# Two masks copied from the identity on VectorE in place of three selects on GpSimd, and one load of x moved from unit 48 of a kernel to its start

## The chip, the cores and the metric

The kernel runs on one core of a Trainium2 chip. The metric is device time in microseconds (us) of one execution; quoted times are medians over several executions, with their number. A profiled execution also gives a span, from the first to the last thing the trace records, which is shorter than the timed figure of the same execution (716.6 beside 718.46 for the kernel before).

Engines: PE is TensorE (matmul), PEld its weight load, DVE VectorE, ACT ScalarE, POOL GpSimd, SP SyncE. An issue is the instruction that starts a transfer; a transfer lands when its last semaphore update is made. A fetch is a transfer that brings the next instructions of an engine's list.

## The reference, cut to what matters

```python
# x (8, 4096, 192) fp32, weight (8 heads, 7 taps), w_in (192, 2048), w_out (2048, 192)
w = softmax(weight, axis=-1)                 # per head
x_pad = six zero rows before each of the 8 sequences
y[b, s, head] = sum_k w[head, k] * x_pad[b, s + k, head]     # causal, depthwise
h = y.reshape(32768, 192) @ w_in
g = where(h > 0, h, exp(min(h, 0)) - 1)      # ELU
out = g @ w_out
```

## The kernel before

The 32768 rows are cut into 32 "supers" of 1024 rows, four to a sequence. Each super has 16 column blocks of w_in, times two halves of 512 rows; one such pair is a "unit", so there are 1024 units. For each unit PE makes H (three matmuls of 512 columns), ACT takes the exponential E of it, POOL clamps E to at most 1, DVE forms gT = max(E - 1, H), and PE multiplies gT into the output banks. The convolution is done for later supers by matmuls with a banded matrix in between. POOL also issues most loads.

GpSimd's program is one list. It makes masks, issues the first loads, and then clamps unit after unit; loads of later x (`x_before`) and the zeroing of the six padding rows at the start of a new sequence (`batch_zeros`) stand between clamps:

```python
X3_AT = (0, 48)     # the two halves of x of super 3: before which unit they are issued
ZERO_AT = 8         # column block in which the padding rows are zeroed
...
for gr in range(2):
    x_before.setdefault(X3_AT[gr], []).append((NXB, gr))
...
g.memset(ones[:], 1.0).then_inc(s_id)
...                                    # ident: one affine_select
for step in range(2):                  # owner: two affine_selects
...                                    # block8: one more
load_w_in(0)                           # three issues each
load_w_in(1)
load_w_out(0)
for gr in range(2):
    load_x(1, gr)
load_w_out(1)
load_w_out(2)
for gr in range(2):
    load_x(2, gr)
for i, (n, u) in enumerate(units):
    s, at_n = divmod(i // 2, NQ)
    if i % 2 == 0 and at_n == ZERO_AT and (s + 2) % SPB == 0 and s + 2 < NS:
        batch_zeros(s + 2)
    for to_load in x_before.get(i, ()):
        load_x(*to_load)
    W(s_exp, i + 1)
    g.tensor_scalar(out=E[:, i % NE, :], in0=E[:, i % NE, :],
                    scalar1=1.0, scalar2=0.0, op0=ALU.min, op1=ALU.max).then_inc(s_clp)
```

The masks are used by the softmax of the weights: `owner` spreads a head's taps over its channels (a matmul on PE), `block8` makes a block diagonal on DVE:

```python
# VectorE, at the start
v.memset(zw[:], 0.0).then_inc(s_zw)
v.memset(wband[:], 0.0).then_inc(s_wb)
v.memset(xbh[:, :, :, :], 0.0).then_inc(s_xz)
W(s_wb, 1)
W(s_wq, 16)                                   # the weights have landed
v.tensor_reduce(wmx[:], wq[:], AXIS.X, ALU.max).then_inc(s_set)
...                                           # subtract, sum, reciprocal, multiply
v.tensor_tensor(wnb[:], block8[:], wn[:, :].unsqueeze(1).to_broadcast([...]), ALU.mult)
```

## Time and profile before

| kernel before | |
|---|---|
| median | 718.48 us (3 executions, 718.13 to 719.18) |
| span of the profiled execution | 716.6 us |
| PE busy | 710.7 us, 99% |
| 62 issues of x loads on POOL | 54.7 us, 884 ns each |
| 1024 clamps on POOL | 603.0 us busy, 611 ns each (they overlap a little, so one per 0.59 us) |

Columns are line, engine, operation, output and input with their shape, count, busy time and mean ns of one, and how long that engine idled before it and for whom.

```profile
L714 POOL TENSOR_SCALAR E<-E 128x512 f32<-128x512 f32 x1024 | 603.0, 611 | 41.1 <-ACT E L760 34.2
L871 DVE SCALAR_TENSOR_TENSOR gT<-E,H 128x512 f16<-128x512 f32 x1024 | 631.8, 681 | 62.8 <-POOL E L714 58.4
```

DVE idles 62.8 us, and 58.4 us of that is waiting for POOL's clamps; POOL itself idles only 41.1 us before its clamps. A unit takes about 0.68 us (1024 units in some 700 us), and POOL can clamp one per 0.59 us (603.0 / 1024), so it has some 0.09 us to spare per unit. Each x issue of 0.88 us therefore puts POOL behind, and by this estimate it needs some 9 or 10 units to catch up.

### The profile page before, as it was taken

The page shows a single profiled execution, that of the slowest core. Times are in us where ns is not written, and L with a number is a line of the kernel's source. Part 1 is how long each engine was busy: PE and PEld are TensorE (multiplying, and loading weights), DVE is VectorE, ACT ScalarE, POOL GpSimd, SP SyncE. Part 2 cuts the span into 40 slices and gives each one's busy share as a digit, 9 for nine tenths or more (in the row PEclk, how much of TensorE's full clock was granted, in tenths as well). Part 3 has the DMA queues.
Part 4 walks back from the last instruction along what each step waited for, and adds up shares of the span by engine and source line. Part 5 has one row for each costly group of instructions (what it writes and reads, how often), then busy time and mean ns, then how long its engine had stood idle before and what let it go on. Part 6 is the DMA issues. An engine that isn't in the chain of part 4 may idle for free.

```text
span 716.6 us, 27662 instructions
## 1 busy us (share of the span) xinstructions
PE 710.7 (99%) x11873; PEld 681.6 (95%) x11873; DVE 641.5 (90%) x1049; ACT 677.4 (95%) x1290; POOL 663.6 (93%) x1112
## 2 busy tenths in 40 slices
PE   8999999999999999999999999999999999999998
PEld 4699999999999999999999999999999999999998
DVE  7999889998898998899998999988989988999994
ACT  6999999999999999999999999999999999999994
POOL 9999999999999999999999999999999999999893
PEclk9999999999999999999999999999999999999999
DMA  9635334564433544444554344544445534444212
GB/s 183 99 72 95 65 73 78 93 86 76 80 79 74 95 89 64 80 85 79 87 91 69 73 76 95 87 73 76 85 73 91 93 63 78 87 80 83 63 43 69
DMA packets 132303, 58.80 MB, mean 82 GB/s; under 512 B 98374, under 2 KB 131412, under 8 KB 132180
## 3 DMA queue, kind: packets, MB, share of 16 engines
q0 software_dynamic: 43504, 16.77, 22.4%
q1 hardware_dynamic: 88388, 39.37, 22.0%
q8 instruction: 93, 1.52, 0.9%
q10 hardware_dynamic: 288, 0.88, 0.4%
q14 instruction: 30, 0.25, 0.1%
HBM read 34.63 MB, written 25.46 MB: 84 GB/s over the span
## 4 chain that ended last, share of the span: by engine, by line
PE 96%; POOL 2%; ACT 1%; DVE 0%; issue 0%; DVEq 0%; POOLq 0%
PE H L1052 54%; PE H L1029 37%; PE H L1004 4%; POOL xg L631 1%; ACT E L760 1%; POOL E L714 1%; POOL w_in L651 0%; POOL w_out L662 0%; DVE gT L871 0%; ACT csb L756 0%; POOL owner L679 0%; DVE osb L862 0%; POOL block L689 0%; POOL ident L668 0%; POOL ones L666 0%
## 5 line engine op out<-in xcount | busy, mean ns | idle before, releaser
L871 DVE SCALAR_TENSOR_TENSOR gT<-E,H 128x512 f16<-128x512 f32 x1024 | 631.8, 681 | 62.8 <-POOL E L714 58.4
L1029 PE MATMUL H<-att,w_in 64*128 64x512 bf16 x3072 | 679.8, 376 | 1.2 <-DVE gT L871 0.9
L1052 PE MATMUL H<-w_out,gT 64*128 64x192 f16 x8192 | 680.4, 243 | 0.1
L714 POOL TENSOR_SCALAR E<-E 128x512 f32<-128x512 f32 x1024 | 603.0, 611 | 41.1 <-ACT E L760 34.2
L1052 PEld LDWEIGHTS H<-w_out,gT 64*128 64x128 f16 x8192 | 606.7, 94 | 17.5 <-PE H L1052 1.5
L760 ACT ACTIVATE E<-H 128x512 f32<-128x512 f32 x1024 | 585.0, 601 | 23.9 <-PE H L1029 0.4
L1029 PEld LDWEIGHTS H<-att,w_in 64*128 64x128 bf16 x3072 | 275.3, 93 | 7.8 <-DVE gT L871 2.9
L1004 PE MATMUL H<-xg,Tm 64*128 64x240 bf16 x496 | 90.9, 263 | 0.0
L756 ACT ACTIVATE csb<-H 112x480 bf16<-112x480 f32 x124 | 70.7, 570 | 0.4 <-PE H L1004 0.3
L767 ACT ACTIVATE osb<-H 128x384 f32<-128x384 f32 (+1 forms) x129 | 62.0, 482 | 6.9 <-PE H L1052 6.8
L631 POOL DMA_DIRECT2D xg<-in_x_dram x62 | 54.7, 884 | 0.2 <-issue 0.2
L1004 PEld LDWEIGHTS H<-xg,Tm 64*128 64x128 bf16 x496 | 42.6, 94 | 1.2 <-DVE gT L871 0.3
L862 DVE COPY osb<-H 128x192 f32<-128x192 f32 x1 | 0.4, 357 | 7.3 <-PE H L1052 7.3
L909 PE MATMUL H<-zw 128*128 128x512 bf16 x10 | 4.3, 588 | 1.2 <-DVE zw L775 1.2
L909 PEld LDWEIGHTS H<-zw 128*128 128x128 bf16 x10 | 1.2, 134 | 3.0 <-issue 1.7
L651 POOL DMA_DIRECT2D w_in<-in_moe_w_in_dram x6 | 3.6, 612 | 0.0
L736 ACT ACTIVATE xb<-xs 128x512 bf16<-128x512 f32 x2 | 1.2, 622 | 2.4 <-DMA xs<-in_x_dram 2.4
L978 PE MATMUL H<-xT,taps 64*64 64x256 bf16 (+1 forms) x50 | 2.6, 317 | 0.0
L662 POOL DMA_DIRECT2D w_out<-in_moe_w_out_dram x3 | 2.5, 853 | 0.0
L978 PEld LDWEIGHTS H<-xT,taps 64*64 64x64 bf16 x50 | 2.0, 106 | 0.5 <-issue 0.2
L729 ACT ACT_TABLE_LOAD x1 | 1.3, 1283 | 1.2 <-PEq L1119 1.2
L936 PEld LDWEIGHTS H<-ident,xb 64*64 64x64 bf16 x48 | 1.2, 126 | 0.8 <-ACT xb L736 0.8
(45 smaller groups left out, 20.5 us busy)
## 6 DMA issues: line engine op xcount, KB each, us to landing
out_dram<-osb SPq DMA_DIRECT2D x126, 192.0 KB, 2.9
xg<-in_x_dram POOLq DMA_DIRECT2D x61, 240.0 KB, 4.5
xs<-in_x_dram ACTq DMA_DIRECT2D x1, 768.0 KB, 4.6
w_in<-in_moe_w_in_dram POOLq DMA_DIRECT2D x6, 128.0 KB, 4.7
att<-csb SPq DMA_TRANSPOSE x31, 3.9
w_out<-in_moe_w_out_dram POOLq DMA_DIRECT2D x2, 192.0 KB, 7.9
w_out<-in_moe_w_out_dram POOLq DMA_DIRECT2D x1, 384.0 KB, 11.8
w_in<-w_in SPq DMA_DIRECT2D x1, 336.0 KB, 6.8
```

The lines of the kernel that those rows point to most:

```text
L631: g.dma_start(xg[0:rows, b, 2 * w0 + gr : 2 * w1 : 2, :], src).then_inc(s_x[b][gr], 16)
L651: g.dma_start(w_in[0:HP, j, c0:c1], bass.AP(tensor=moe_w_in.tensor, offset=8 * j * FF + c0, ap=[[CPH * FF, HEADS], [FF, 8], [1, c1 - c0]], ...
L714: g.tensor_scalar(out=E[:, i % NE, :], in0=E[:, i % NE, :], scalar1=1.0, scalar2=0.0, op0=ALU.min, op1=ALU.max,).then_inc(s_clp)
L756: a.activation(*conv_evac(W, m), ACT.Copy).then_inc(s_ce)
L760: a.activation(E[:, i % NE, :], H[:, bank_of[item], :], ACT.Exp).then_inc(s_exp)
L767: a.activation(*out_evac(W, *item[1:]), ACT.Copy).then_inc(s_oev[item[2]])
L871: v.scalar_tensor_tensor(out=gT[:, s % NG3, q, u, :], in0=E[:, i % NE, :], scalar=1.0, in1=H[:, bank_of[item], :], op0=ALU.subtract, op1=A ...
L909: pe.matmul(H[:, bank, :], zw[:, 0:P], zw[:, 0:GS], start=True, stop=True)
L978: ins = pe.matmul(H[to, bank_of["d", j] + (j == 2 and c0 > 0), c0:c1], taps[rows, tap, rows], xT[rows, j, HALO - PAD + tap + c0 : HALO - P ...
L1004: ins = pe.matmul(H[:, bank_of["c", m], 256 * q : 256 * q + UC], Tm[rows, h, :], xg[rows, s % NXB, :, CPH * h : CPH * (h + 1)].rearrange(" ...
L1029: ins = pe.matmul(H[:, bank_of[item[:3]], :], w_in[HP * r : HP * (r + 1), j, FC * q : FC * (q + 1)], att[HP * r : HP * (r + 1), s % 2, j, ...
L1052: ins = pe.matmul(acc_of(k, g)[:, D * kb : D * (kb + 1)], gT[HP * rt : HP * (rt + 1), t % NG3, q, g, t0 : t0 + P], w_out[HP * rt : HP * (r ...
```

## The change

The intent: POOL's list at the start sets when the first clamp happens, so take three mask selects off it. `owner` and `block8` are both repeats of the 8 x 8 corner of the identity, so VectorE copies them from there, before the weights have landed. In the room gained, the second half of x of super 3 is issued at the start, so that no x issue stands at unit 48.

```diff
@@ -41,7 +41,7 @@
 WCOLS = ((0, 8 * FC), (8 * FC, 16 * FC))
 UPPER = ((0, FC), (FC, 2 * FC), (2 * FC, 4 * FC), (4 * FC, 8 * FC), (8 * FC, 16 * FC))
 WOUT = (0, 4, 8, 16)
-X3_AT = (0, 48)
+X3_AT = (0, 0)
 HALO = 8
 BW = P
 ON_DVE = 3
@@ -466,6 +466,7 @@
         s_scr = sema("s_scr")
         s_x = [[sema(f"s_x{i}_{g}") for g in range(2)] for i in range(NXB)]
         s_id = sema("s_id")
+        s_own = sema("s_own")
         s_xs = sema("s_xs")
         s_xh = sema("s_xh")
         s_wb = sema("s_wb")
@@ -674,27 +675,6 @@
                 base=0,
                 channel_multiplier=1,
             ).then_inc(s_id)
-            for step in range(2):
-                W(s_id, 2 + step)
-                g.affine_select(
-                    out=owner[:, :],
-                    in_=owner[:, :] if step else ones[0:HEADS, :],
-                    pattern=[[0, 2], [1 - 2 * step, HP]],
-                    compare_op=ALU.is_ge,
-                    fill=0.0,
-                    base=7 * step,
-                    channel_multiplier=8 * (2 * step - 1),
-                ).then_inc(s_id)
-            W(s_id, 4)
-            g.affine_select(
-                out=block8[:, :, :],
-                in_=ones[0:HEADS, 0 : HEADS * KSIZE].rearrange("p (h k) -> p h k", h=HEADS),
-                pattern=[[1, HEADS], [0, KSIZE]],
-                compare_op=ALU.is_equal,
-                fill=0.0,
-                base=0,
-                channel_multiplier=-1,
-            ).then_inc(s_id)
             load_w_in(0)
             load_w_in(1)
             load_w_out(0)
@@ -775,6 +755,18 @@
             v.memset(zw[:], 0.0).then_inc(s_zw)
             v.memset(wband[:], 0.0).then_inc(s_wb)
             v.memset(xbh[:, :, :, :], 0.0).then_inc(s_xz)
+            W(s_id, 2)
+            v.tensor_copy(
+                owner[:, :].rearrange("p (g h e) -> p g h e", g=2, e=8),
+                ident[0:HEADS, 0:HEADS]
+                .unsqueeze(1)
+                .unsqueeze(3)
+                .to_broadcast([HEADS, 2, HEADS, 8]),
+            ).then_inc(s_own)
+            v.tensor_copy(
+                block8[:, :, :],
+                ident[0:HEADS, 0:HEADS].unsqueeze(2).to_broadcast([HEADS, HEADS, KSIZE]),
+            ).then_inc(s_own)
             W(s_wb, 1)
             W(s_wq, 16)
             v.tensor_reduce(wmx[:], wq[:], AXIS.X, ALU.max).then_inc(s_set)
@@ -798,7 +790,7 @@
                 scalar2=None,
                 op0=ALU.mult,
             ).then_inc(s_set)
-            W(s_id, 5)
+            W(s_own, 2)
             W(s_set, 5)
             v.tensor_tensor(
                 wnb[:],
@@ -908,7 +900,7 @@
                     for _ in range(item[2]):
                         pe.matmul(H[:, bank, :], zw[:, 0:P], zw[:, 0:GS], start=True, stop=True)
                 elif item[0] == "s":
-                    W(s_id, 4)
+                    W(s_id, 2)
                     W(s_set, 6)
                     pe.matmul(
                         H[:, bank_of["d", 2], 0:KSIZE],
```

## The prediction

> **What bounds the kernel now.** I read four views of the kernel before, in this order: the busy shares of the page, the chain of waits over the whole span, the same chain in its first 46 us, and the matmul counts in stretches of 1 us around the one place where the chain leaves the PE late.
>
> First the page: busy shares, then the chain that ended last.
>
> ```profile
> PE 710.7 (99%) x11873; PEld 681.6 (95%) x11873; DVE 641.5 (90%) x1049; ACT 677.4 (95%) x1290; POOL 663.6 (93%) x1112
> ...
> PE 96%; POOL 2%; ACT 1%; DVE 0%; issue 0%; DVEq 0%; POOLq 0%
> ```
>
> The PE is busy 99% of the 716.6 us and carries 96% of the chain. Cut into stretches of 100 us between 100 and 600 us, it executes 1695 to 1697 matmuls in each and is never idle. So the middle of the kernel is a fixed amount of matmul work, and nothing in this change touches its matmuls. Only the 4% of the chain that is not PE can be won, and that lies at the two ends. What POOL has of the chain is in the first 46 us; columns are start, duration and what ran:
>
> ```profile
> 1.07 0.30 POOL ident L668
> 1.43 0.30 POOL owner L679
> 1.79 0.30 POOL owner L679
> 2.14 0.33 POOL block L689
> 2.48 0.73 POOL w_in L651
> ...
> 10.15 2.69 POOL xg L631 x3
> 12.86 0.64 POOL E L714
> 13.52 0.70 DVE gT L871
> 14.27 1.45 PE H L1029 x7
> ...
> 40.98 1.77 POOL E L714 x3
> 42.74 0.82 POOL xg L631
> 43.59 0.64 POOL E L714
> 44.26 0.70 DVE gT L871
> 45.00 0.28 PE H L1029
> ```
>
> Two things are to be seen. At the start the chain is POOL's own program, one item behind the other: four masks, then twelve issues of transfers, until POOL is free for the first clamp of E at 12.86. The PE then goes on at 14.27. At 42.74 the chain passes through POOL once more: one issue of x for super 3 (its second half) stands between two clamps, gT comes late and the PE's next H matmul waits for its bank until 45.00. After that the chain stays on the PE until the tail.
>
> What the second place costs I take from the counts of matmuls that touch each microsecond: H matmuls (512 columns) first, then the output matmuls (192 columns). The stretches are the same, 43 to 47.
>
> ```profile
> 43.00:44.00 1.00, 1.00 (x6) 1.00 0.55 184
> 44.00:45.00 1.00, 0.50 (x4) 1.00 0.82 85
> 45.00:46.00 1.00, 1.00 (x5) 1.00 1.33 156
> ...
> 43.00:44.00 1.00, 1.00 (x15) 1.00 0.55 184
> 44.00:45.00 1.00, 0.78 (x11) 1.00 0.82 85
> 45.00:46.00 1.00, 0.78 (x9) 1.00 1.33 156
> ```
>
> The convolution matmuls (240 columns) are 0, 2 and 2 there. In columns: 6 x 512 + 15 x 192 = 5952 in the full microsecond, 4 x 512 + 11 x 192 + 2 x 240 = 4640 in the next, 5 x 512 + 9 x 192 + 2 x 240 = 4768 in the third. Missing: 1312 + 1184 = 2496 of 5952 per us, which is 0.42 us of PE work. It is never made up, because the PE has no idle time afterwards.
>
> **What the Trainium skill says.** "DMA: Bandwidth & Descriptors", section "SWDGE vs HWDGE vs iDMA": a transfer issued from GpSimd has its descriptors computed in software on that engine. The trace agrees that this is POOL time: the 62 issues of xg take 884 ns each, the three in a row before the first clamp 2.73 us, 0.91 each. The same page, section "Queues, rings and completion order": one DMA engine alternates between its queues, and switches only after a whole packet of descriptors. That bears on w_in beside the first load of x; the trace of before cannot settle it, because the packets of the x load run from 1.84 to 5.04 and those of w_in only begin at 3.95. "SBUF — State Buffer", section "Who interferes with whom": a VectorE copy in a two-port mode locks GpSimd out for the whole instruction, descriptor writing included. The first w_in issue took 777 ns and the next five 562 to 600, beside small VectorE work; this fits, but does not prove it.
>
> **The change part by part.**
>
> Removed from POOL: three mask selects, from the start of the first at 1.43 to the first w_in issue at 2.43. That is 1.00 us. Nothing else stands there: POOL is not waiting for anything from 0.79 to 12.86.
>
> Moved on POOL: the issue of the second half of super 3 goes from before unit 48 (42.68) to before unit 0. It adds one issue, 0.91 us by the spacing of its neighbours. Net on POOL at the start: -1.00 + 0.91 = -0.09 us, so the first clamp comes at about 12.77. DVE, then PE, follow with the spacings of before, and the chain from there to 40 us is PE and ACT work with no wait for a transfer, so I let 0.1 us through to the end.
>
> At unit 48: ACT takes the exponential of this unit at 42.10. Where POOL is free, the clamp follows an exponential at 0.67 us after its start (ACT 24.07 to POOL 24.74), so at 42.77. POOL's clamps before it end by 42.74. So unit 48 goes at about 42.77 in place of 43.59, gT at 43.43 and the bank is free at 44.17 in place of 45.00. The PE finishes the work in front of it (two convolution matmuls from 44.01 and 44.12) about then, so the stall should go almost whole: -0.4 us. It cannot give the full 0.82 us of the issue, since the PE lost only 0.42.
>
> Added on DVE: two copies of 8x128 and 8x56 elements. Small DVE instructions follow each other here at 0.19 us (wmx 2.25, the subtraction 2.44); I take 0.22 each, 0.44 in all. DVE idles 0.26 us for the weights before wmx, so the softmax moves by about 0.2 us. It leads through taps and x to the first attention tile, the first H (10.55) and the first exponential (11.39). That last one could feed POOL at 11.39 + 0.67 = 12.06, and POOL will not be free until 12.77: 0.7 us of slack, more than 0.2. So it costs nothing at the end.
>
> The instructions and waits of PE, ACT and SP are the same in both kernels but for the PE's wait for the masks. Sum: -0.1 - 0.4 = -0.5 us, 718.48 - 0.5 = 718.0.
>
> **The rivals.**
>
> First: the earlier w_in issue slows the first load of x. ACT waits for that load until 5.44, and everything up to the first exponential hangs on it. For: w_in's issue comes 1.0 us sooner, at 1.4, while this 768 KB load is running. Against: the slack of 0.7 us, minus the 0.2 used by the masks. If the load slips by 1.0 us, the start gets 0.5 us worse, and the time is about 718.5.
>
> Second: the copies on VectorE hold up POOL's descriptor writing, or the thirteenth issue takes longer with so many transfers queued. Each would eat the net 0.09 and perhaps 0.3 more: 718.1 to 718.4.
>
> Third: the issue at 42.68 is hidden, or another wait takes its place. For: ACT is busy almost throughout (4.88 of 5 us between 40 and 45) and has no lead of its own to give. Against: ACT itself waited 0.31 us for the PE at 45.44, so ACT was then held up by this stall and not its cause. If it were so, 718.4.
>
> Fourth: the 240 KB added to the opening backlog of transfers, which drains at 24.84, lengthen it by about 1.3 us (super 3's first half took 190 GB/s there) to 26.1. The first transpose of attention is issued at 25.70 and lands at 29.94. I expect at most tenths, since the added load is last in its queue and w_out and super 1 and 2 stand before it.
>
> **Range and chances.** All four rivals move tenths of a microsecond; three runs of before lie from 718.13 to 719.18, so the noise is of the size of the gain. Without any gain and with high noise, 718.9; with both gains whole and low noise, 717.2. Two per cent is 14.4 us; nothing here is larger than 2 us. So: within 2% 0.98, 0.01 on each side.
>
> **What would show each step.** Right: the first w_in issue near 1.4; four xg issues in a row before a first clamp near 12.8; no gap of POOL, and no DVE idle of 0.75 us, near 43 to 44; PE counts without the dip at 44 to 46; steady counts of 1695 per 100 us as before; span about 716.1. Wrong: a first clamp later than 12.9 (second rival; or the first, if its idle time is put down to ACT), ACT waiting for x beyond 5.7, the same dip with another releaser (third), or attention landing later than 30.2 (fourth). If the PE is idle at a new place after 50 us, my claim that it is saturated falls.

## More of the kernel before

The output of each group of 256 or 128 rows is copied from its bank to SBUF and stored. SyncE issues every store but the last, ScalarE the last one; the copy before that one is on VectorE:

```python
# SyncE
elif item[1:] != (NK - 1, 1):
    evacuated_by(W, *item[1:])
    out_group(sy, *item[1:])
# ScalarE, after everything else
evacuated_by(W, NK - 1, 1)
out_group(a, NK - 1, 1)
```

## The result, and the profile after

| | before | changed |
|---|---|---|
| median | 718.40 us (6 executions, 718.13 to 719.18) | 719.06 us (6 executions, 718.46 to 719.57) |
| span of the profiled execution | 716.61 us | 717.00 us |

The ratio of times is 1.0008, with a 95% interval of 0.9995 to 1.0021. So the class, within 2%, was right; 719.06 lies outside the predicted range of 717.2 to 718.9, and the gain of 0.5 us is not there.

The two parts that the change aimed at did what they should. First the chain of waits of the changed kernel at the start (start, duration, what ran):

```profile
1.45 0.78 POOL w_in L652
...
9.15 3.41 POOL xg L632 x4
12.56 0.73 POOL E L694
13.32 0.70 DVE gT L863
14.06 1.45 PE H L1021 x7
```

The first w_in issue starts at 1.45 in place of 2.43. There are four x issues in a row, and then the first clamp at 12.56, against 12.86. PE goes on at 14.06, against 14.27: 0.21 us earlier, where 0.09 had been worked out.

The counts of H matmuls per microsecond at unit 48 (stretch, busy time of all, busy time and count of these matmuls, granted clock, DMA share, GB/s):

```profile
43.00:44.00 1.00, 1.00 (x6) 1.00 0.55 181
44.00:45.00 1.00, 0.95 (x5) 1.00 0.05 11
45.00:46.00 1.00, 1.00 (x6) 1.00 0.00 0
```

The output matmuls in the second of these microseconds:

```profile
44.00:45.00 1.00, 0.93 (x13) 1.00 0.05 11
```

With the four convolution matmuls there, it has 5 x 512 + 13 x 192 + 4 x 240 = 6016 columns, where before it had 4640. The dip is gone, and in the timeline of POOL the eight clamps there run without a break:

```profile
40.78 4.85 POOL L694 TENSOR_SCALAR E<-E 128x512 f32<-128x512 f32 x8 [0.29 <-ACT E L740]
```

To see where the gain went, the busy shares are of no use, since PE is busy 99% in both. What helps is that both kernels execute the same 11760 matmuls, from the first H on, in the same order but for neighbours. I took the start times of each from the two traces and subtracted. This is output of my own, not a view of the profile; negative means that the changed kernel is ahead:

```
at us (before's time)   changed minus before, us
19 to 43                -0.20
47 to 63                -0.63
66 ... 588              loses some 0.04 (0.03 to 0.06) at each of 66, 153, 240, 327, 414, 501, 588
last matmul starts      -0.34     (713.43 before, 713.09 changed)
span ends               +0.39     (716.61 before, 717.00 changed)
from last matmul to end  3.18 before, 3.92 changed
```

So the gain of 0.63 was there at 63 us. Then 0.29 of it was given back in seven small steps over the middle, and the last 3 us of the kernel, after the last matmul has started, became 0.73 longer. In sum: -0.20 - 0.43 + 0.29 + 0.73 = +0.39 us.

The last copy out of PSUM on VectorE, with its start, shows that the lead still existed there. First before, then changed:

```profile
713.81 0.36 DVE L862 COPY osb<-H 128x192 f32<-128x192 f32 x1 [7.34 <-PE H L1052]
```

```profile
713.47 0.36 DVE L854 COPY osb<-H 128x192 f32<-128x192 f32 x1 [7.34 <-PE H L1044]
```

It is 0.34 earlier, and yet the kernel ends 0.39 later. What lies between is only the last stores. The DMA view of 714 to 717 us shows them: the busy tenths of the 16 DMA engines and the rate in 40 slices of 75 ns, and the queues with packets, MB and share. Before:

```profile
DMA  9999999511799637999999400000000000000000
GB/s 379 379 358 379 349 358 359 164 31 72 246 389 369 195 103 256 348 399 349 349 369 328 144 21 0 0 0 0 0 0 0 0 0 0 0 0 0 0 0 0
```

Changed:

```profile
DMA  9999999971699999999983100000000000000000
GB/s 358 348 389 379 349 359 379 328 232 31 215 348 328 338 389 348 359 318 348 389 287 103 41 20 21 20 20 21 0 0 0 0 0 0 0 0 0 0 0 0
...
q14 instruction: 1, 0.01, 0.8%
```

The changed kernel has a transfer there that the other has not: one fetch of instructions of 8 KB, on queue 14, at 714.66 us, 391 ns long on its DMA engine. In the kernel before the same fetch comes at 717.7, after the last store. In both kernels the store that is issued and lands last is one of SyncE's, on queue q1 (q10 has ScalarE's, and its last packet ends sooner). It was issued at 714.26 before and at 714.32 in the changed kernel. The last sixteen semaphore updates of the stores came from 715.97 to 716.14 before, and from 715.91 to 716.53 in the changed kernel: the first of them earlier, the last of them late. The kernel waits for the last. The rates show how it was late: before, they fall from 328 to 0 within three slices; in the changed kernel five slices of 20 or 21 GB/s follow at the end, about a sixteenth of the 320 to 390 of the slices before. One of the 16 DMA engines, it seems, was still at work alone. In the trace itself the last packets end one by one, 33 ns apart, for the last 0.3 us; before, the last 24 end within 0.1 us.

The Trainium skill, "DMA: Bandwidth & Descriptors", section "Queues, rings and completion order", puts instruction refills on row 14 of the same DMA engines that serve the data rows, and says that an engine takes turns between its rows, packet by packet. The trace agrees on the queue number for this fetch, though queue 8, too, carries packets of instructions (93 in the kernel before). The last store, issued 0.05 us later than before, landed 0.39 us later, and the 0.34 us between fit one DMA engine that was held up for the length of the fetch. The trace does not name the engine of a packet, so that it is the one with the fetch is inferred. "Runtime: NRT & Kernel Launch", section "Instruction fetch mechanics", says that each engine prefetches its stream in fixed blocks and that its cost is mostly hidden. Whether it is so here, in the tail, the experiments have to show.

### The profile page after: what moved, and what is told of

Its sections match the earlier page's. It is cut to its first block, busy times and chain, and to the rows that moved or that the text cites. A ratio compares the mean times of both kernels' runs of the same rounds, so it can differ in the third digit from the quotient of the medians.

```text
span 717.0 us, 27661 instructions
## 1 busy us (share of the span) xinstructions
PE 710.5 (99%) x11873; PEld 682.4 (95%) x11873; DVE 642.5 (90%) x1051; ACT 677.4 (94%) x1290; POOL 663.3 (93%) x1109
## 3 DMA queue, kind: packets, MB, share of 16 engines
q8 instruction: 93, 1.52, 0.9%
## 4 chain that ended last, share of the span: by engine, by line
PE 97%; POOL 2%; ACT 1%; DVE 0%; issue 0%; DVEq 0%; POOLq 0%
PE H L1044 55%; PE H L1021 38%; PE H L996 4%; POOL xg L632 1%; POOL w_in L652 0%; ACT E L740 0%; POOL w_out L663 0%; DVE gT L863 0%; POOL E L694 0%; ACT csb L736 0%; DVE osb L854 0%; POOL ident L669 0%; POOL ones L667 0%; DVEq L513 0%; POOLq L1111 0%
```

## The experiments

Eleven kernels were run. Medians compare with the kernel before of the same rounds: 718.56 for the first four, 718.78 for the next four, 718.53 for the last three. None of them is more than 2% from it; the differences that they are to tell apart are below 1 us, so most verdicts rest on the matmul start times and landings of the traces.

### 1. The kernel before once more, as a null

No edit.

> The kernel before, unchanged, against itself: the null. Both theories: ratio 1.0000, and the interval shows what size of difference can be seen at all. Theory T (the output transfers at the very end set the span, and they vary from run to run): last matmul of the profiled run at 713.4 us within 0.1, while the time from the last matmul to the end (3.2 us in the first profile) varies by some tenths. Theory C (a half-speed spell of the TensorE clock near the end costs the time): runs listed with clock 0.999 are slower by 0.3 us or more than those with 1.000, here too.

Measured: 718.81 us (5 executions, 718.50 to 720.03), ratio 1.0008 [0.9995, 1.0020]. A kernel compared with itself gave the ratio of the change. The five executions span 1.5 us. The slowest of them is the profiled one, so its cause can be seen. Windows of 15 to 20 us (stretch, then busy time and instruction counts of PE, PEld, DVE, ACT, POOL, granted clock, DMA share, GB/s), first the kernel before as profiled at first, then this execution:

```profile
15.00:20.00 5.00, 4.94 (x54) 2.89 (x54) 5.00 (x9) 4.46 (x9) 5.00 (x10) 1.00 1.39 250
```

```profile
15.00:20.00 5.00, 4.94 (x36) 2.65 (x37) 5.00 (x9) 3.37 (x7) 4.57 (x9) 0.66 1.43 241
```

PE did 36 matmuls in place of 54 with a granted clock of 0.66, and its matmuls are 1.46 to 1.51 us late from there to the end. A spell at half speed of about 3.4 us gives 0.66 over 5 us ((1.6 + 3.4/2)/5). The Trainium skill, "TensorE: Matmul & The Clock Gate", section "What's actually happening", describes a gate that gives half rate after an idle window of about 3.4 us, and a window that runs freely, so that the moment varies from run to run; the trace agrees in length (the clock record has half rate from 16.64 to 20.05). An idle window before it is not to be seen: PE was busy for 4.02 us from 10 to 15 us, against 3.99 in the execution that kept its clock. What follows: a single execution can be 1.5 us late for no reason of the kernel, and the time of the change could not be judged from the six executions alone.

### 2. The changed kernel once more

No edit.

> The changed kernel once more. Theory T: the matmuls start 0.62 us sooner than in the kernel before by 60 us of the span and 0.3 to 0.6 us sooner at the last one, in this profile too; the span doesn't follow, because the last issue of SP comes after 714.2 us again. Ratio 1.0000 to 1.0010. Theory C: the ratio follows the share of runs with clock 0.999. Theory N (no difference, the first six runs were unlucky): ratio below 1.0000.

Measured: 718.58 us (5 executions, 718.49 to 718.94), ratio 1.0002 [0.9988, 1.0016]. Matmul starts: -0.01 up to 43 us, -0.44 after unit 48, -0.13 for the last matmul, and 3.53 us from there to the end. The start of the kernel thus varies by 0.2 us between executions, the step of -0.43 at unit 48, the loss of 0.31 over the middle and the longer end repeat. The fetch falls at 714.7 here too. Part of the first 719.06 was chance: the same kernel gave 718.58 here. But the predicted 0.5 us is missing in both. A suspicion that the executions with a mean granted clock of 0.999 were the long ones did not hold: here the executions at 0.999 took 718.58 and 718.88, those at 1.0 took 718.49 to 718.94. In the first six of the changed kernel it had held, though: the three at 0.999 took 719.16 to 719.57, the other three 718.46 to 718.95. Whether they had spells as in run 1 cannot be seen, since only one execution of each kernel left a trace.

### 3. Only the x load moved

```diff
-X3_AT = (0, 48)
+X3_AT = (0, 0)          # in the kernel before; masks stay on POOL
```

> Only the second half of super 3's x moved to the start; masks stay on POOL. By the prediction's sums: first clamp at 12.86 + 0.91 = 13.8, so PE 0.9 us later at 14 to 40 us, then 0.42 won at unit 48: last matmul 0.5 us later than before, 713.9, ratio 1.0007 if the end follows the PE. Theory T: the end doesn't follow the PE by tenths, ratio anywhere from 1.000 to 1.001.

Measured: 719.20 us (5 executions, 719.10 to 719.31), ratio 1.0009 [0.9996, 1.0021]. Matmul starts: +0.98 up to 43 us, +0.55 after, +0.87 for the last matmul, 3.07 us to the end. The added issue at the start costs about its own length (0.9) when no mask is taken away for it. The stall at unit 48 goes, -0.43, and then the lead shrinks by 0.32 over the middle, without any change to the masks. The end is as short as before and the fetch comes at 718.5, after it.

### 4. Only the masks moved

```diff
-X3_AT = (0, 0)          # in the changed kernel
+X3_AT = (0, 48)
```

> Only the masks moved to VectorE; the second half of super 3 stays before unit 48. By the prediction's sums POOL would be free at 11.9, but the first exponential now comes at 11.81 in the changed kernel, so the clamp can begin at 12.5 at the soonest: 0.35 us won at the start, and the stall at 44 to 46 us stays (0.42 lost). Last matmul 0.2 to 0.35 us sooner than before. Theory T: time within 0.05% of before.

Measured: 718.80 us (5 executions, 718.61 to 720.32), ratio 1.0009 [0.9996, 1.0021]. Matmul starts: -0.38 up to 43 us, -0.37 after, -0.36 for the last matmul: no loss in the middle. At the start ScalarE now sets the pace: the first exponential came at 11.81, and the first clamp at 12.50, although POOL's last issue ended at 11.71. But it is 3.83 us from the last matmul to the end, with the fetch at 714.6.

This splits the two losses cleanly. The loss in the middle comes with the x load (runs 2 and 3, not 4). The longer end comes with the masks (runs 2 and 4, not 3).

### 5. Two idle instructions on VectorE

If the longer end has to do with where VectorE's instruction stream is cut for fetching, then any two more instructions there must do it, and what they do must not matter.

```diff
+pad = sbuf("pad", [HEADS, 2], FP32)      # in the kernel before
 v.memset(xbh[:, :, :, :], 0.0).then_inc(s_xz)
+for i in range(2):
+    v.memset(pad[:, i : i + 1], 0.0)
```

> The kernel before plus two one-element memsets on VectorE at the start: nothing of the change but its two more VectorE instructions. Theory F (the tail of the changed kernel is longer because with two more VectorE instructions an 8 KB instruction fetch, which in the kernel before comes after the end of the span, falls at 714.6 us, among the last output transfers): that fetch comes at 714 to 715 us, the landings of the last output group spread over 0.4 us or more in place of 0.17, the time from the last matmul to the end grows from 3.2 to 3.5 us or more, with the last matmul at 713.4 as before. Rival T2 (the tail grows because the PE ends sooner while the transfers have a floor of their own): the tail stays at 3.2 us.

Measured: 719.20 us (4 executions, 718.93 to 719.74) against 718.78, ratio 1.0006 [0.9991, 1.0021]. Matmul starts: +0.13 throughout, no loss in the middle. 3.54 us from the last matmul to the end. The DMA view of 714 to 717 us has the fetch, at 715.0 us:

```profile
q14 instruction: 1, 0.01, 1.0%
```

and the last sixteen updates of the stores came from 716.01 to 716.62. So two instructions that nobody reads, in the first 2 us of the kernel, bring the fetch among the last stores 713 us later, and with it the longer end.

### 6. The masks copied by ScalarE

```diff
 # ScalarE, after the exponential of the softmax
+W(s_id, 2)
+a.activation(owner..., ident[0:HEADS, 0:HEADS]..., ACT.Copy).then_inc(s_own)
+a.activation(block8..., ident[0:HEADS, 0:HEADS]..., ACT.Copy).then_inc(s_own)
 # VectorE: the two tensor_copy taken out again
```

> The changed kernel with the two mask copies on ScalarE, so that VectorE's instructions are those of the kernel before. Theory F: no fetch between 712 and 716 us unless ScalarE's own two instructions bring one; tail 3.1 to 3.3 us, so the span is 716.2 to 716.5 with the last matmul at 713.1 to 713.3. Rival T2: tail 3.5 to 3.9, span 716.8 or more.

Measured: 718.45 us (4 executions: 718.24, 719.53, 718.30, 718.59), ratio 1.0000 [0.9983, 1.0017]. Matmul starts: -0.20, -0.63, -0.35 for the last matmul, as in the changed kernel, and 3.20 us to the end in place of 3.92. Span 716.28, 0.72 us under that of the changed kernel. The fetch comes at 717.4, after the end. With VectorE's instruction count as before, the end is as before. This is the counterpart of run 5: the same work on another engine has not the cost. (A run with so many more VectorE instructions that the fetch falls before the stores was not made; it would have parted the fetch from the count.)

### 7. One of the last stores issued by ScalarE

In the changed kernel's trace SyncE's second store issue of the tail takes 1547 ns, against 1142 before, so its last one leaves at 714.32 although the copy was done at 713.69. That was the rival for the longer end: SyncE, not the fetch.

```diff
 # ScalarE, after its copy of group (NK - 2, 1)
+if item[1:] == (NK - 2, 1):
+    evacuated_by(W, NK - 2, 1)
+    out_group(a, NK - 2, 1)
 # SyncE
-elif item[1:] != (NK - 1, 1):
+elif item[1:] not in ((NK - 2, 1), (NK - 1, 1)):
```

> The changed kernel with one of the last output transfers issued by ScalarE in place of SyncE. Theory T (SyncE's row of issues holds the last output back: it issued it at 714.32 though it was evacuated at 713.69): SyncE's last issue by 713.9, tail shorter by 0.3 us or more, span 716.3 to 716.7. If only the fetch holds the end (theory F alone), the last issue comes sooner but the last landing still spreads, and the span stays within 0.2 us of 716.8 to 717.0.

Measured: 719.06 us (4 executions, 718.78 to 719.23) against 718.78, ratio 1.0003 [0.9988, 1.0018]. SyncE's last issue now left at 713.83, half a microsecond sooner, and still the last packet landed at 716.47, 3.75 us from the last matmul to the end, with the fetch at 714.7. So here SyncE's issues are not what holds the end. In the changed kernel's first profile they are a part of it, and the traces say how large. The end has three parts: from the start of the last matmul to the last issue of a store, from there to its landing, and from the landing to the end of the span, which is 0.47 or 0.48 in all profiles. Before, the first two were 0.83 and 1.87 us; in the changed kernel they were 1.23 and 2.21. So 0.40 of the 0.73 is SyncE's late last issue, and 0.34 is the slower landing. The first repeats only in run 4 (1.17). It is not in run 2, which is the same kernel and where SyncE's second issue took 902 ns and not 1547; why this issue varies is open. The slower landing is in all six profiles with the fetch in the tail, and it grows with the fetch: the table under "What the runs show together" has both.

### 8. The x issue at unit 29

The x issue must stand somewhere. Is there a place in the middle that hides it?

```diff
-X3_AT = (0, 0)          # in the changed kernel
+X3_AT = (0, 29)
```

> The changed kernel with the second half of super 3's x issued before unit 29 in place of before unit 0. Drift theory (every later issue of xg takes 892 to 895 ns in place of 882 in all kernels that issue this one among the first transfers, and the PE pays about 0.3 us for it in all): here the later issues take 882 ns and the matmul starts keep their lead from 60 us on to the end. The start is as with the masks alone, 0.36 to 0.38 us ahead of the kernel before. At unit 29 the engines run at ScalarE's pace and not the PE's: if the issue is hidden there, the lead at 60 us is 0.8; if not, 0.0 to 0.4. Rival (the drift belongs to a PE that runs ahead): 882 ns but the lead shrinks all the same.

Measured: 720.43 us, one execution, its state unknown. Matmul starts: +0.79 at first, +1.55 between 35 and 43 us, +1.11 after unit 48, +1.39 for the last matmul. So the issue cost 0.76 at unit 29, more than the 0.43 that it costs at unit 48. The +0.79 at the start is no effect of the edit that I can name: PE's first 32 transposes took 1.47 us in place of 0.86, as at half clock, but the clock record of this trace begins only at 10 us, so this is not shown. The loss of 0.28 over the middle is there again. It tells against what I had thought to be its cause, the duration of POOL's later x issues, which is the next point.

### 9. The zeroing of the padding moved by four column blocks

The seven losses are 87 us apart, which is four supers, one sequence. Once per sequence POOL has one instruction more than otherwise: the memset of the six padding rows. The timeline of POOL in run 6, at the second loss (start, duration, line, operation, count):

```profile
149.04 0.89 POOL L632 DMA_DIRECT2D xg<-in_x_dram  x1
149.97 1.77 POOL L694 TENSOR_SCALAR E<-E 128x512 f32<-128x512 f32 x3
151.68 0.25 POOL L647 MEMSET xg<- 6x192 bf16 x1
151.90 4.15 POOL L694 TENSOR_SCALAR E<-E 128x512 f32<-128x512 f32 x7
```

It stands three clamps after an x issue. There POOL is still catching up, and 0.25 us are added to what it has to catch up. The edit, on top of run 6, puts it elsewhere:

```diff
-ZERO_AT = 8
+ZERO_AT = 12
```

> The mask copies on ScalarE, x as in the changed kernel, and the memset of each batch's padding on POOL four units of 16 later (before step 12 and not 8), out of the stretch in which POOL catches up after an issue of xg. Theory P (in that stretch POOL and VectorE set the pace of the PE, once per batch, so 10 ns more per xg issue are paid by the PE there): the slips of 0.035 us at 153, 240, 327, 414, 501 and 588 us vanish, the lead of 0.63 us at 60 us holds to within 0.1 at the end, last matmul at 712.8 or sooner. Rival (the slip is the PE's own, it comes with running ahead): the lead shrinks to 0.35 again, last matmul 713.1. Tail 3.2 us if no fetch falls in it, so a span of 716.0; ratio to the kernel before 0.9985 to 0.9995.

Measured: 717.68 us (5 executions, 717.57 to 717.75) against 718.53 (9 executions, 718.32 to 718.79), ratio 0.9989 [0.9976, 1.0001]. Every execution lies under every one of the kernel before. Matmul starts: -0.19, -0.62, and -0.72 for the last matmul: the lead no longer shrinks, it grows, so the kernel before paid a little at these places too. The same stretch of POOL now runs on:

```profile
149.94 4.65 POOL L694 TENSOR_SCALAR E<-E 128x512 f32<-128x512 f32 x8
154.80 1.19 POOL L694 TENSOR_SCALAR E<-E 128x512 f32<-128x512 f32 x2 [0.20 <-ACT E L754]
```

and POOL idles 0.20 us after eight clamps, so it has caught up. In the kernels with the loss, POOL's clamps and DVE's gT carry the same new offset as PE from each of the seven places on.

This settles where the middle's loss is paid. It does not settle why it is larger with the x load moved. The one difference that I found is that the 53 x issues between 60 and 640 us are longer. Durations are min/median/max in ns, then first and last start; before, then changed:

```profile
L631 POOL DMA_DIRECT2D xg<-in_x_dram x53: 869/882/885, 62.6 to 628.5; - x53
```

```profile
L632 POOL DMA_DIRECT2D xg<-in_x_dram x53: 879/894/897, 62.0 to 628.2; - x53
```

Run 4, without the loss, has a median of 882; runs 3, 6 and 9 have 894. That fits, but run 8 has 884 and loses 0.28 all the same, and a longer issue by 12 ns is less than the some 40 ns lost each time. So the duration is at most a part of it. What makes the issues longer, and what the rest is, stays open.

### 10. Run 9 with the store of run 7

```diff
 # run 9, and ScalarE issues the store of group (NK - 2, 1) as in run 7
```

> The same, and one of the last output transfers issued by ScalarE. With no fetch among the last transfers SyncE's row of issues is what is left of the tail: its last issue comes at once after the evacuation, 0.1 to 0.2 us sooner, tail 3.0 to 3.1 us. Rival: the last landing doesn't move, tail 3.2.

Measured: 717.59 us (5 executions, 717.51 to 717.82), ratio 0.9988 [0.9976, 1.0001]. 3.00 us from the last matmul to the end, against 3.18 in run 9; the difference of the times, 0.09, cannot be told from chance.

### 11. Run 6 once more

No edit to run 6, since its four executions had been spread over 1.3 us.

> The changed kernel with the mask copies on ScalarE once more, timed with more rounds. Theory F: last matmul 713.1, tail 3.2 us, ratio below 1.0000 (0.9993 to 0.9999). If the first profile's 716.3 was luck: ratio 1.000 or above, as the changed kernel's.

Measured: 718.11 us (5 executions, 718.09 to 718.45) against 718.53, ratio 0.9997 [0.9983, 1.0011]. Matmul starts: -0.21, -0.65, -0.37, and 3.07 to the end. So run 6 holds in the trace: what was left of the predicted gain once the fetch is out of the way, about 0.4 us. The medians differ by as much (0.42), but the interval of the ratio includes 1. Run 9 beside it, on the same chip in the same rounds, is another 0.43 under it, with all five executions under all five of run 11.

### What the runs show together

"Last matmul" is the start of the last matmul against that of the kernel before's first profile; "end" is from there to the end of the span. "To issue" is from the start of the last matmul to the last issue of a store, "landing" from that issue to its landing.

| run | last matmul | end, us | to issue | landing | fetch on queue 14 at (its length) |
|---|---|---|---|---|---|
| before | 0 | 3.18 | 0.83 | 1.87 | 717.7, after the end |
| 1 before again | +1.51 | 3.23 | 1.00 | 1.76 | 719.3, after the end |
| 3 x only | +0.87 | 3.07 | 0.77 | 1.82 | 718.5, after the end |
| 6 masks on ScalarE | -0.35 | 3.20 | 0.82 | 1.91 | 717.4, after the end |
| 9 and zeroing moved | -0.72 | 3.18 | 0.77 | 1.93 | 717.0, after the end |
| 10 and a store moved | -0.57 | 3.00 | 0.77 | 1.76 | 716.9, after the end |
| 11 run 6 again | -0.37 | 3.07 | 0.77 | 1.82 | 717.2, after the end |
| changed | -0.34 | 3.92 | 1.23 | 2.21 | 714.66 (0.39) |
| 4 masks only | -0.36 | 3.83 | 1.17 | 2.19 | 714.6 (0.39) |
| 5 two idle instructions | +0.12 | 3.54 | 0.77 | 2.30 | 715.0 (0.48) |
| 2 changed again | -0.13 | 3.53 | 0.77 | 2.28 | 714.7 (0.50) |
| 8 x at unit 29 | +1.39 | 3.78 | 0.77 | 2.53 | 716.3 (0.67), span ends 718.6 |
| 7 changed, a store moved | -0.23 | 3.75 | 0.77 | 2.50 | 714.7 (0.68) |

The seven runs without the fetch in the tail end in 3.00 to 3.23 us, the six with it in 3.53 to 3.92. The fetch comes 4.1 to 4.3 us after the start of the last matmul in the first kind and 1.4 to 1.6 us after it in the second. The first kind has VectorE's instruction count of the kernel before, the second two more.

The landing takes 1.84 us in the mean of the seven. In the six it takes 0.35 to 0.69 us more, and each time this excess is the length of the fetch to within 0.06 us (0.37 and 0.35 beside 0.39, 0.46 beside 0.48, 0.44 beside 0.50, 0.69 beside 0.67, 0.66 beside 0.68). In all six the last packets of the stores end one by one, 33 ns apart, for the last 0.3 us; in all seven others the last 24 end within 0.11 us. That the count goes with the longer end is shown by runs 5 and 6; that the fetch is what does it rests on this agreement in size.

## Why the prediction was wrong

Two steps failed: that the masks on VectorE cost nothing at the end, where the last store landed 0.34 us later for a fetch that their two instructions moved there; and that the middle of the kernel cannot change, where 0.29 us of the lead was lost. Another 0.40 us of the first profile, SyncE's late last issue, is a matter of the single execution. Point by point, by the prediction's own steps.

- **POOL at the start.** Right in kind and direction: three selects gone, the first w_in issue 0.98 us earlier, four x issues and then the clamp. The net was larger, -0.30 at the first clamp and -0.20 to -0.21 on PE in the first profile, and -0.01 in the second. Executions differ here by more than the term. The list counts "twelve issues of transfers" where its own lines have fourteen, so the added one is the fifteenth and not the thirteenth; no sum rests on it.
- **Unit 48.** Right, in mechanism and size: -0.42 was read from the matmul counts, and -0.43 was measured in the changed kernel and in runs 2, 3, 6 and 11. That they agree to 0.01 is luck, since the counts take a matmul into every microsecond that it touches.
- **The masks on VectorE.** The step said that they cost nothing at the end, by slack at the start. At the start that is so: the copies run at 1.92 and 2.00 us in the gap before the weights land, and the next instruction starts at 2.23, against 2.25. At the end of the kernel it was wrong. That those two instructions lengthen VectorE's stream was stated in effect ("Added on DVE: two copies"), but only their time was counted. By moving a fetch among the last stores (runs 5 and 6) they made the landing of the last store 0.34 us longer than before in the changed kernel, and 0.35 to 0.69 longer in the six runs than in the mean of the other seven: the size of the whole predicted gain.
- **The middle.** The other step that failed is "nothing in this change touches its matmuls", with "It is never made up, because the PE has no idle time afterwards". Equal counts of 1695 to 1697 per 100 us cannot show a loss of 0.04 us, the sixth part of one output matmul of 243 ns. PE is paced by POOL for a moment once per sequence, where the memset meets the catching up after an x issue; there +0.29 was given back. The lines that hint at it are POOL's 41 us and DVE's 58 us of waits, shown above.
- **The rivals.** The first happened in small: ACT's first use of x began at 5.60 in place of 5.44, inside the slack. But the slack was less than the 0.7 us of the prediction: the first exponential came at 11.81 in place of 11.39, so a clamp could start at about 12.48, and POOL was free at 12.56. In run 4 this limit is what held the start. The second did not show at the first clamp: its four x issues took 3.41 us, against 2.69 for three. And the first w_in issue, which the prediction set beside VectorE's work, took 777 ns in all thirteen profiles, whatever VectorE did: it does not speak for a lock. The third is refuted by the counts. The fourth did not happen: the first transpose of attention was issued at 25.49 and took 4.1 us to land, against 25.70 and 4.2. None of the four was the cause, because all four were sought before 50 us.
- **The sum.** -0.20 - 0.43 was right, against -0.5 predicted. What is missing is +0.29 in the middle and +0.73 at the end (0.34 the landing, 0.40 SyncE's issue). On top, the first six executions seem to have been high by chance: five more of the same kernel gave 718.58, inside the range, but without the predicted gain.
- **The chances.** "Within 2%" was safe and right. The range took its width from the executions of before, and had no term for the end of the kernel.

The kernel of run 9 is the better one: 717.68 against 718.53 for the kernel before, with all its five executions under all nine of that, though the interval of the ratio just reaches 1 (1.0001). Its gain is the predicted one, plus the loss in the middle undone, without the fetch.

## What to carry to other kernels

When the gain looked for is a few tenths of a microsecond, compare the start times of the same instructions in both traces over the whole span: this shows at once where a lead is won and where it is lost again, which busy shares and counts cannot. Count what lies after the last matmul too, because there nothing hides a fetch of instructions or a late packet, and an instruction added at the start of an engine's list can move it. A busy PE is not proof that no other engine paces it: look at the engine with little slack per unit, and keep its extra instructions apart from each other.

## What the Trainium skill lacked or had wrong

- "Runtime: NRT & Kernel Launch", section "Instruction fetch mechanics", calls the cost of fetching mostly hidden and says nothing of the end of a kernel. Here one fetch of 391 ns at 714.66 us, beside the last stores, and its like in five other runs came with a last store that took 2.19 to 2.53 us to land in place of 1.76 to 1.93; two added VectorE instructions (run 5) brought it there.
- The same section gives 16 KiB as the block of a refill. The queues here show two sizes: q8 has 93 packets with 1.52 MB, 16 KB each, and q14 has 30 packets with 0.25 MB, 8 KB each. (Whether a packet is a whole block, the trace does not say.)
- "DMA: Bandwidth & Descriptors" calls the making of descriptors small in its section "Anatomy of one DMA". An x issue of 240 KB held POOL for 884 ns in the mean of 62 (the issue as a whole; the trace does not split it), and it is this that cost 0.43 us at unit 48 and 0.76 at unit 29.
- No page has it that the duration of these issues differs between kernels with the same issue: a median of 882 ns before and 894 after one of them had been moved to the start. Its cause is open.
